# A fused attention and MLP kernel: four slots for the copies of q sums in two batches, and the loads of weights issued from ACT's queue

## The chip, the cores and the metric

The kernel runs on one core of one Trainium2 chip, as one launch. A core has five engines that each work through instructions of their own in program order and meet at semaphores: TensorE (PE in the profile, with its loads of stationary operands as PEld), VectorE (DVE), ScalarE (ACT), GpSimd (POOL) and SyncE (SP), and 16 DMA engines that the queues of the issuing engines feed. The metric is the device time of the launch in microseconds; less is better.

## The reference

Linear attention with exponential features, and then an MLP of two matmuls with a GELU between, in fp32:

```python
def phi(x):                      # q, k: 8 batches, 8 heads, 576 positions, 64 wide
    proj = einsum('bhsd,df->bhsf', x, w_phi)                 # 128 features
    proj = proj - max(abs(proj), axis=-1, keepdims=True)
    return concatenate([exp(proj), exp(-proj)], axis=-1)

kv  = einsum('bhsf,bhsd->bhfd', phi(k), v)
z   = sum(phi(k), axis=2)
num = einsum('bhsf,bhfd->bhsd', phi(q), kv)
den = einsum('bhsf,bhf->bhs', phi(q), z)[..., None] + 1e-06
x   = (num / den), heads side by side                        # 4608 tokens x 512
out = gelu(x @ w_in) @ w_out                                 # 512 -> 2048 -> 512
```

`w_in` and `w_out` are float64, so they reach the chip as 8-byte words and are made into fp32 there.

## The kernel before, in words

**Attention.** A batch is worked in two quads of four heads (`k_quad`, L379) and four pairs of heads (`q_pair`, L459). A quad loads `kt` and `vt`, and for each of five units PE projects k into `pk`, DVE takes the largest absolute value (`mx`, L417) and subtracts it, ACT makes the two exponentials `ek` (L433), and PE adds their products with v up in `kv`, which ACT copies to `kvn`. A pair, for each half of the positions, loads `qt`, projects it to `pq`, ACT copies it to `pc`, GpSimd finds the largest absolute value over the features (`mb`, L499), DVE subtracts it, and ACT makes `ef` (L505). In the first two batches (`b < ND`) PE then computes, for each of the two heads, 65 rows `pn` out of `ef` and `kvn` (64 of the numerator, one of the denominator). ACT copies them to `xo` (L515), and two DMAs write them from there to DRAM, `x_d` (L517) and `d_d` (L519). In later batches the denominator goes through `un` and `db` (L529 to L535) and one copy takes both heads. `quotients` reads the denominators of a half back, inverts them and writes `r_d`.

**MLP.** `block` (L578) takes 256 tokens: it loads `xr` from `x_d` and `rb` from `r_d`, multiplies, splits the product into `xh` and `xl`, and then alternates three matmuls per piece of `w_in` into `ph`, two GELUs on ACT, a difference on DVE (`gl`) and three matmuls per piece of `w_out` into `po`. There are 18 blocks.

**Weights.** 32 tiles of 128 x 512 eight-byte words, 512 KB each, go through `split_weight` (L330). One DMA brings `raw` (L336). ACT takes the absolute value of the upper words (`wt`, L339), DVE clamps, shifts and joins in four steps (L340 to L346), ACT casts the result to `w`, and DVE subtracts for the remainder. `raw` and `w` have a tag of their own each time, so no load waits for a slot; `weights` (L355) lets load number n be issued from n x 3.996 us on in the plan.

**Order.** Each operation is handed to a planner with `op(engine, cost, function, reads, writes, rank)`. `order` (L105) plays a list schedule in which an engine takes, of the operations that could start now, the one of the least rank; the slots of SBUF and PSUM are part of it (a tag has n buffers, taken in turn). `emit` (L240) writes the instructions out in the order of their planned starts. On the chip each engine then keeps that order, and waits where something is late. The first two batches have ranks from -200, the weights from 43.9 on, the blocks from 57.4 on.

Slots of the tags that matter here: `xo` 2, `un` 1, `db` 1 in SBUF (L288), `pn` 1 in PSUM (L290).

Of the kernel before, what the change touches and what calls it, by code (L numbers as in the profile page):

```python
# [10 lines left out]
F32 = mybir.dt.float32  # L11
F32R = mybir.dt.float32r
U32 = mybir.dt.uint32
I64 = mybir.dt.int64
# [13 lines left out]
P = 128  # L28
HS = S // 2
# [29 lines left out]
class Plan:  # L59
# [19 lines left out]
    def op(self, eng, cost, fn, r=(), w=(), also=(), rank=0.0, table=None, late=0.0, kb=0, duty=1.0, kind="f", psum=False):  # L79
        o = Op()  # L80
        o.eng, o.cost, o.fn, o.rank, o.table, o.late, o.n = eng, cost, fn, rank, table, late, len(self.ops)
        o.users, o.ready, o.nbytes, o.duty, o.kind, o.psum = [], self.since, kb, duty, kind, psum
        deps = set()
        for b in r:
            deps.update(b.writers)
        for b in w:
            deps.update(b.writers)
            deps.update(b.readers)
        for b in r:
            b.readers.append(o)  # L90
        for b in w:
            b.writers.append(o)
        o.bufs = list(dict.fromkeys([*r, *w, *also]))
        for b in o.bufs:
            b.left += 1
        o.deps = deps
        o.wait = len(deps)
        for d in deps:
            d.users.append(o)
        if eng == "pe" and self.stream in ("k", "q"):  # L100
            o.rank += PULL
        self.ops.append(o)
        return o

    def order(self, bias):  # L105
# [54 lines left out]
        while len(done) < n:  # L160
# [33 lines left out]
            _, t, o = best  # L194
# [14 lines left out]
            if o.eng == "pool":  # L209
                taken.append([t, t + cost, False])  # L210
            o.start, o.end = t, run(t, cost, o.duty) if o.eng == "pe" else t + cost
            if o.nbytes:
                dge[0] = max(dge[0], t) + 0.55
                dma[0] = max(dma[0], dge[0] + 0.75) + o.nbytes / 350.0
                o.late = dma[0] + 0.15 - o.end
# [60 lines left out]
def fused_kernel(ctx: ExitStack, tc: tile.TileContext, qT, kT, va, w_st, w_in, w_out, out):  # L276
# [53 lines left out]
    def split_weight(src, nm, rank):  # L330
        tag = f"w_{nm}"
        raw = plan.pool(spool, tag, 1)([P, 512, 2], U32, f"raw_{nm}")
        w = plan.pool(spool, tag, 1)([P, 2, 512], F32R, f"w_{nm}")
        t = sb["ob"]([P, 512], U32, f"wt_{nm}")
        k = dict(rank=rank)
        op("sp", 0.06, lambda: nc.sync.dma_start(out=raw().bitcast(I64), in_=src), w=[raw], kb=524, **k)  # L336
        low, high = (lambda: raw()[:, :, 0]), (lambda: raw()[:, :, 1])
        v = nc.vector
        op("act", act(512) + 0.04, lambda: nc.scalar.activation(t().bitcast(F32), high().bitcast(F32), AF.Abs), r=[raw], w=[t], **k)  # L339
        op("dve", dve(512, fast=True), lambda: v.tensor_scalar(  # L340
            out=t().bitcast(F32), in0=t().bitcast(F32), scalar1=F64_MIN, scalar2=F64_MAX, op0=ALU.max, op1=ALU.min), r=[t], w=[t], **k)
        op("dve", dve(512, fast=True), lambda: v.tensor_scalar(
            out=t(), in0=t(), scalar1=3, scalar2=0x3FFFFFF8, op0=ALU.logical_shift_left, op1=ALU.bitwise_and), r=[t], w=[t], **k)
        op("dve", dve(512), lambda: v.scalar_tensor_tensor(  # L344
            out=t(), in0=low(), scalar=29, in1=t(), op0=ALU.logical_shift_right, op1=ALU.bitwise_or), r=[raw, t], w=[t], **k)
        op("dve", dve(512), lambda: v.scalar_tensor_tensor(  # L346
            out=t(), in0=high(), scalar=0xC0000000, in1=t(), op0=ALU.bitwise_and, op1=ALU.bitwise_or), r=[raw, t], w=[t], **k)
        hi = lambda: w()[:, 0, :]
        copy("act", act(512), hi, lambda: t().bitcast(F32), [t], [w], **k)
        tt("dve", dve(512), lambda: w()[:, 1, :], lambda: t().bitcast(F32), lambda: hi().bitcast(F32), ALU.subtract, [t, w], [w], **k)  # L350
        return w
# [107 lines left out]
    def q_pair(b, p, kvs, rank, halves=(0, 1)):  # L459
# [4 lines left out]
        for half in halves:  # L464
# [43 lines left out]
            if b < ND:  # L508

                for j in range(2):  # L510
                    pn = ps["pn"]([P, HS], F32, f"pn_{nm}_{j}")
                    op("pe", 2 * mm4_cost(D + 1, HS), lambda pn=pn, kvn=kvn, ef=ef, j=j: [
                        mm(pn()[: D + 1], lhsT=kvn()[:, 2 * s + j, :], rhs=ef()[:, s, j], start=s == 0, stop=s == 1) for s in range(2)
                    ], r=[kvn, ef], w=[pn], kind="d", **k())
                    xo = sb["xo"]([P, HS], F32, f"xo_{nm}_{j}")  # L515
                    copy("act", act(HS, True), lambda xo=xo: xo()[: D + 1], lambda pn=pn: pn()[: D + 1], [pn], [xo], **k())
                    op("sp", 0.06, lambda xo=xo, x_to=x_to, j=j: nc.sync.dma_start(out=x_to()[64 * j : 64 * j + 64], in_=xo()[:D]),  # L517
                       r=[xo], w=[x_to], kb=74, **k())
                    op("sp", 0.06, lambda xo=xo, d_to=d_to, j=j: nc.sync.dma_start(out=d_to()[2 * p + j : 2 * p + j + 1], in_=xo()[D : D + 1]),  # L519
                       r=[xo], w=[d_to], kb=1, **k())  # L520
                continue
# [167 lines left out]
EPACE = 20.0  # L689
TF = 90.0  # L690
ND = 2
LUMP = 2.5
LINGER = 3.0
PAIR_K = 0.43
# [48 lines left out]
```

## Time and profile before

| | us |
|---|---|
| median of 3 runs | 1156.19 |
| the three runs | 1152.53, 1156.19, 1345.22 |
| the profiled execution | 1154.29 |
| its span, first to last instruction | 1152.5 |
| PE busy in the span | 1114.6 |
| ACT busy | 570.2 |
| DVE busy | 547.5 |
| POOL busy | 317.8 |

Busy times are of the whole span; the opening, in which the weights come in and the first two batches are worked, differs from the rest, so a table by stretches is read beside the page. An instruction that issues a DMA is not counted as busy. Every DMA of this kernel is issued by SP, and the profile tells the length of the issue, not the time until the data has landed. The granted clock is the share of TensorE's full clock that it had in a stretch.

### The profile page before, as it was taken

What the parts mean: (1) busy time and instruction counts of PE and PEld (TensorE: products, weight loads), DVE (VectorE), ACT (ScalarE), POOL (GpSimd) and SP (SyncE); (2) the same over time, 40 slices, a digit from 0 to 9 for tenths busy, and PEclk for the clock granted to TensorE, in tenths of its full rate; (3) what the DMA queues carried; (4) which work ended last, traced back from release to release, by engine and by line L of the source; (5) the groups of instructions that cost most, each with busy time, mean ns of one, the idle gap of its engine ahead of it and who ended that gap; (6) DMA issues with size and microseconds to landing.
All of it is one profiled execution on the core that took longest, in us unless ns stands there. A gap on an engine that the chain in (4) does not pass through costs nothing.

```text
span 1152.5 us, 21902 instructions
## 1 busy us (share of the span) xinstructions
PE 1114.6 (97%) x9096; PEld 930.4 (81%) x9096; DVE 547.5 (48%) x905; ACT 570.2 (49%) x965; POOL 317.8 (28%) x116
## 2 busy tenths in 40 slices
PE   7887999999999999999999999999999999999998
PEld 4554777887887888878888878888899998989997
DVE  5987898454556464444465455545211212122010
ACT  4877667555555565657556555555322222222121
POOL 3323023263435243333453543343300000000000
PEclk8999999999999999999999999999999999999999
DMA  7778623223141413222231321212012011010000
GB/s 264 218 218 240 196 67 84 83 74 101 34 123 50 117 33 108 72 73 73 79 106 56 111 65 32 76 35 76 22 47 55 8 48 48 8 38 19 1 19 19
DMA packets 80852, 92.00 MB, mean 80 GB/s; under 512 B 24736, under 2 KB 67904, under 8 KB 80752
## 3 DMA queue, kind: packets, MB, share of 16 engines
q1 hardware_dynamic: 80752, 90.60, 26.9%
q8 instruction: 71, 1.16, 0.4%
q14 instruction: 29, 0.24, 0.1%
HBM read 71.40 MB, written 19.17 MB: 79 GB/s over the span
## 4 chain that ended last, share of the span: by engine, by line
PE 75%; DVE 4%; POOL 2%; issue 1%; ACT 1%; DMA 0%; SPq 0%; ACTq 0%; POOLq 0%; DVEq 0%
PE po L295 32%; PE ph L295 30%; PE kv L295 4%; PE pn L295 4%; PE pq L295 2%; PE pk L295 2%; POOL mb L499 1%; DVE pc L321 1%; POOL db L534 1%; DVE gl L321 1%; DMA rb<-r_d 0%; DVE mx L417 0%; DVE wt_o L344 0%; ACT pc L315 0%; DVE wt_o L346 0%
## 5 line engine op out<-in xcount | busy, mean ns | idle before, releaser
L295 PE MATMUL ph<-xh,w_i 128*128 128x256 f32 x2304 | 433.8, 283 | 0.5 <-DVE gl L321 0.5
L295 PEld LDWEIGHTS ph<-xh,w_i 128*128 128x128 f32 x2304 | 362.4, 189 | 11.2 <-issue 3.5
L295 PE MATMUL po<-w_o,gh 128*128 128x512 f32 x1152 | 364.8, 398 | 0.0
L295 PE MATMUL ph<-xl,w_i 128*128 128x256 f32 x1152 | 323.7, 281 | 0.0
L321 DVE TENSOR_TENSOR gl<-ph,gh 128x512 fp32r<-128x512 f32 x144 | 98.9, 688 | 326.3 <-ACT ph L622 325.6
L295 PEld LDWEIGHTS po<-w_o,gh 128*128 128x128 f32 x1152 | 209.5, 188 | 48.8 <-ACT gh L621 2.4
L534 POOL PARTITION_ALL_REDUCE db<-un x48 | 175.2, 3649 | 224.7 <-DVE un L531 137.1
L295 PE MATMUL po<-w_o,gl 128*128 128x512 f32 x576 | 229.3, 398 | 6.8 <-DVE gl L321 6.5
L499 POOL PARTITION_ALL_REDUCE mb<-pc x64 | 144.1, 2252 | 281.2 <-ACT pc L315 215.2
L295 PEld LDWEIGHTS ph<-xl,w_i 128*128 128x128 f32 x1152 | 217.6, 189 | 2.8
L621 ACT ACTIVATE gh<-ph 128x512 fp32r<-128x512 f32 x144 | 86.1, 598 | 267.7 <-PE ph L295 267.2
L295 PEld LDWEIGHTS po<-w_o,gl 128*128 128x128 f32 x576 | 108.0, 188 | 37.9 <-DVE gl L321 13.7
L433 ACT ACTIVATE ek<-pk 128x512 f32<-128x512 f32 (+1 forms) x160 | 81.0, 553 | 72.4 <-DVE pk L321 70.9
L295 PEld LDWEIGHTS kv<-vt,ek 128*64 128x64 f32 (+1 forms) x2560 | 85.3, 139 | 35.4 <-ACT ek L433 15.0
L295 PE MATMUL kv<-vt,ek 128*64 128x65 f32 (+1 forms) x2560 | 97.7, 227 | 12.3 <-ACT ek L433 11.1
L295 PE MATMUL pn<-ef,kvn 128*64 128x288 f32 (+1 forms) x512 | 98.0, 425 | 9.9 <-ACT xo L315 7.1
L417 DVE TENSOR_REDUCE mx<-pk 128x4 f32<-128x512 f32 (+1 forms) x80 | 50.5, 632 | 112.8 <-PE pk L295 112.8
L505 ACT ACTIVATE ef<-pc 128x576 f32<-128x576 f32 x128 | 82.2, 681 | 29.6 <-DVE pc L321 29.0
L622 ACT ACTIVATE ph<-ph 128x512 f32<-128x512 f32 x144 | 85.4, 593 | 0.0
L321 DVE TENSOR_TENSOR pc<-pc,mb 128x576 f32<-128x576 f32 x64 | 57.6, 900 | 52.9 <-POOL mb L499 52.6
L295 PEld LDWEIGHTS pn<-ef,kvn 128*64 128x64 f32 (+1 forms) x512 | 38.9, 138 | 45.5 <-ACT xo L315 11.8
L621 ACT ACT_TABLE_LOAD x48 | 61.6, 1283 | 27.0 <-PE ph L295 26.4
(47 smaller groups left out, 768.5 us busy)
## 6 DMA issues: line engine op xcount, KB each, us to landing
qt<-in_qT_dram SPq DMA_DIRECT2D x112, 144.0 KB
vt<-in_va_dram SPq DMA_DIRECT2D x16, 585.0 KB
kt<-in_kT_dram SPq DMA_DIRECT2D x16, 576.0 KB
out_dram<-ob SPq DMA_DIRECT2D x36, 256.0 KB
raw_i<-in_w_in_dram SPq DMA_DIRECT2D x16, 512.0 KB
raw_o<-in_w_out_dram SPq DMA_DIRECT2D x16, 512.0 KB
x_d<-xo SPq DMA_DIRECT2D x48, 144.0 KB
x_d<-xo SPq DMA_DIRECT2D x32, 72.0 KB
```

What stands on the lines that cost most here:

```text
L295: return tc.keep_in_program_order(nc.tensor.matmul(*a, **kw))
L321: op(eng, cost, lambda: e.tensor_tensor(out=dst(), in0=a(), in1=b(), op=o), r=r, w=w, **kw)
L417: op("dve", dve(256 * n, True), lambda xs=xs, mx=mx: nc.vector.tensor_reduce(out=mx()[:, 0].rearrange("p (j i) -> p j i", j=2), in_=xs(), ...
L433: op("act", act(256 * n, True), lambda xs=xs, es=es, s=s: nc.scalar.activation(es[s](), xs(), AF.Exp, scale=1.0 - 2.0 * s), r=[x], w=[e[s] ...
L499: op("pool", 2.2, lambda mb=mb, pc=pc: nc.gpsimd.partition_all_reduce(mb(), pc(), P, bass_isa.ReduceOp.absmax), r=[pc], w=[mb], **k(1))
L505: op("act", act(2 * HS), lambda ef=ef, pc=pc, s=s: nc.scalar.activation(ef()[:, s], pc(), AF.Exp, scale=1.0 - 2.0 * s), r=[pc], w=[ef], ta ...
L534: op("pool", 3.7, lambda db=db, un=un: nc.gpsimd.partition_all_reduce(db(), un(), P, bass_isa.ReduceOp.add), r=[un], w=[db], **k())
L621: op("act", act(2 * TB, True) + 0.016, lambda gh=gh, ph=ph: nc.scalar.activation(gh(), ph(), AF.Gelu), r=[ph], w=[gh], table="gelu", rank= ...
L622: op("act", act(2 * TB, True) + 0.037, lambda ph=ph: nc.scalar.activation(ph(), ph(), AF.Gelu), r=[ph], w=[ph], table="gelu", rank=URGE + rk)
```

## The change

The copies `xo` of the first two batches take their slot in turn from the tags `xo`, `un`, `xo`, `db`, four buffers instead of two, with no new memory. The 32 loads of weights are issued by ACT (`nc.scalar.dma_start`) instead of SP, with a planned cost of 0.1 and a rank that is lower by 300. The planner takes such a load to land a fixed time after its issue, and it takes no share of the planned DMA queue any more.

```diff
--- before.py
+++ after.py
@@ -209,7 +209,9 @@
             if o.eng == "pool":
                 taken.append([t, t + cost, False])
             o.start, o.end = t, run(t, cost, o.duty) if o.eng == "pe" else t + cost
-            if o.nbytes:
+            if o.nbytes and o.eng == "act":
+                o.late = 2.0 + o.nbytes / 150.0
+            elif o.nbytes:
                 dge[0] = max(dge[0], t) + 0.55
                 dma[0] = max(dma[0], dge[0] + 0.75) + o.nbytes / 350.0
                 o.late = dma[0] + 0.15 - o.end
@@ -333,7 +335,7 @@
         w = plan.pool(spool, tag, 1)([P, 2, 512], F32R, f"w_{nm}")
         t = sb["ob"]([P, 512], U32, f"wt_{nm}")
         k = dict(rank=rank)
-        op("sp", 0.06, lambda: nc.sync.dma_start(out=raw().bitcast(I64), in_=src), w=[raw], kb=524, **k)
+        op("act", ISSUE, lambda: nc.scalar.dma_start(out=raw().bitcast(I64), in_=src), w=[raw], kb=524, rank=rank - 300.0)
         low, high = (lambda: raw()[:, :, 0]), (lambda: raw()[:, :, 1])
         v = nc.vector
         op("act", act(512) + 0.04, lambda: nc.scalar.activation(t().bitcast(F32), high().bitcast(F32), AF.Abs), r=[raw], w=[t], **k)
@@ -512,7 +514,7 @@
                     op("pe", 2 * mm4_cost(D + 1, HS), lambda pn=pn, kvn=kvn, ef=ef, j=j: [
                         mm(pn()[: D + 1], lhsT=kvn()[:, 2 * s + j, :], rhs=ef()[:, s, j], start=s == 0, stop=s == 1) for s in range(2)
                     ], r=[kvn, ef], w=[pn], kind="d", **k())
-                    xo = sb["xo"]([P, HS], F32, f"xo_{nm}_{j}")
+                    xo = sb[("xo", "un", "xo", "db")[(2 * half + j) % 4]]([P, HS], F32, f"xo_{nm}_{j}")
                     copy("act", act(HS, True), lambda xo=xo: xo()[: D + 1], lambda pn=pn: pn()[: D + 1], [pn], [xo], **k())
                     op("sp", 0.06, lambda xo=xo, x_to=x_to, j=j: nc.sync.dma_start(out=x_to()[64 * j : 64 * j + 64], in_=xo()[:D]),
                        r=[xo], w=[x_to], kb=74, **k())
@@ -689,6 +691,7 @@
 EPACE = 20.0
 TF = 90.0
 ND = 2
+ISSUE = 0.1
 LUMP = 2.5
 LINGER = 3.0
 PAIR_K = 0.43
```

The planner makes a new order from that, on every engine. Three places of it follow. Names end in a running number that has no meaning; `pc_0_0_1` is batch 0, pair 0, half 1, `ek_0_0_0_1` is batch 0, quad 0, unit 0, sign 1, `raw_i0_0` is a tile of `w_in`, and the lines of the change stand two higher than before.

ACT at the start of the program, before:

```order
L300 ACTIVATE idle_66<-idle_66 128x1
L315 COPY pc_0_0_0_106<-pq_0_0_0_0_95 128x288
L315 COPY pc_0_0_0_106<-pq_0_0_0_1_97 128x288
L433 ACTIVATE ek_0_0_0_1_127<-pk_0_0_0_101 128x512
L315 COPY pc_0_0_1_131<-pq_0_0_1_0_120 128x288
L315 COPY pc_0_0_1_131<-pq_0_0_1_1_122 128x288
L433 ACTIVATE ek_0_0_0_0_137<-pk_0_0_0_101 128x512
L433 ACTIVATE ek_0_0_1_140<-pk_0_0_1_111 128x512 x2
L505 ACTIVATE ef_0_0_0_162<-pc_0_0_0_106 128x576 x2
L339 ACTIVATE wt_i0_0_173<-raw_i0_0_82 128x512
L339 ACTIVATE wt_i1_0_183<-raw_i1_0_91 128x512
```

and now:

```order
L338 DMA raw_i0_0_70<-in_w_in_dram 128x512
L302 ACT_TABLE_LOAD
L302 ACTIVATE idle_66<-idle_66 128x1
L338 DMA raw_i1_0_91<-in_w_in_dram 128x512
L341 ACTIVATE wt_i0_0_94<-raw_i0_0_70 128x512
L338 DMA raw_i2_0_105<-in_w_in_dram 128x512
L317 CAST w_i0_0_112<-wt_i0_0_94 128x512
L317 COPY pc_0_0_0_116<-pq_0_0_0_0_100 128x288
L317 COPY pc_0_0_0_116<-pq_0_0_0_1_102 128x288
L341 ACTIVATE wt_i1_0_125<-raw_i1_0_91 128x512
L317 COPY pc_0_0_1_138<-pq_0_0_1_0_131 128x288
L317 COPY pc_0_0_1_138<-pq_0_0_1_1_133 128x288
```

The first load and the whole conversion of its tile now stand ahead of the first copy `pc`, two more loads are issued before it, and the second conversion begins between the copies of the two halves.

SP where the copies of batch 1 are written out and the first block's `xr` is read (`vt_2_1` is an input of batch 2), before:

```order
L517 DMA x_d1_1_1_1171<-xo_1_1_1_1_1201 64x288
L519 DMA d_d1_1_1038<-xo_1_1_1_1_1201 1x288
L336 DMA raw_o11_1231<-in_w_out_dram 128x512
L469 DMA qt_1_3_1_1240<-in_qT_dram 128x288
L591 DMA xr_0_1188<-x_d0_1_0_445 128x256
L595 DMA rb_0_1190<-r_d0_0_861 64x4x256
L517 DMA x_d1_2_0_1283<-xo_1_2_0_0_1270 64x288
L519 DMA d_d1_0_986<-xo_1_2_0_0_1270 1x288
L336 DMA raw_i0_3_1290<-in_w_in_dram 128x512
L388 DMA vt_2_1_1294<-in_va_dram 128x1170
L591 DMA xr_0_1188<-x_d0_2_0_614 128x256
```

and now:

```order
L519 DMA x_d1_1_1_1206<-xo_1_1_1_0_1201 64x288
L521 DMA d_d1_1_1076<-xo_1_1_1_0_1201 1x288
L471 DMA qt_1_3_0_1215<-in_qT_dram 128x288
L597 DMA rb_0_1174<-r_d0_0_889 64x4x256
L593 DMA xr_0_1172<-x_d0_2_0_664 128x256
L519 DMA x_d1_1_1_1206<-xo_1_1_1_1_1231 64x288
L521 DMA d_d1_1_1076<-xo_1_1_1_1_1231 1x288
L390 DMA vt_2_1_1278<-in_va_dram 128x1170
L593 DMA xr_0_1172<-x_d0_3_0_797 128x256
L471 DMA qt_1_3_1_1290<-in_qT_dram 128x288
L519 DMA x_d1_2_0_1325<-xo_1_2_0_0_1320 64x288
```

The loads of weights between the writes and reads are gone, and the fourth read of `xr_0` now comes ahead of the writes of `xo_1_2`, behind three of which it stood before.

PE where the first matmuls of block 0 stand (`ph_0_0`, `pn_1_3` is the last pair of batch 1), before:

```order
L295 MATMUL kv_2_0_0_1313<-vt_2_0_956,ek_2_0_1_1_1391 64x65 x2
L295 MATMUL pn_1_3_0_1_1426<-ef_1_3_0_1379,kvn_1_1_1_1296 65x288 x2
L295 MATMUL pk_2_0_2_1438<-wst_68,kt_2_0_868 128x128 x2
L295 MATMUL pn_1_3_1_0_1446<-ef_1_3_1_1431,kvn_1_1_1_1296 65x288 x2
L295 MATMUL ph_0_0_1456<-xh_0_1429,w_i0_0_260 128x256
```

and now:

```order
L297 MATMUL kv_2_0_0_1380<-vt_2_0_957,ek_2_0_0_1_1318 64x65 x2
L297 MATMUL kv_2_0_0_1380<-vt_2_0_957,ek_2_0_0_0_1351 64x65 x2
L297 MATMUL kv_2_0_0_1380<-vt_2_0_957,ek_2_0_0_1_1318 64x65 x2
L297 MATMUL pk_2_0_1_1410<-wst_68,kt_2_0_867 128x128 x4
L297 MATMUL ph_0_0_1419<-xh_0_1339,w_i0_0_112 128x256
```

`ph_0_0` stood behind three of the four groups `pn_1_3`; now it and `ph_0_1` stand ahead of all four.

## Rows read from the trace of the kernel before

**Rows 1.** The page, busy time of each engine (us, share of the span, instructions).

```profile
PE 1114.6 (97%) x9096; PEld 930.4 (81%) x9096; DVE 547.5 (48%) x905; ACT 570.2 (49%) x965; POOL 317.8 (28%) x116
```

**Rows 2.** Table by stretches: length, busy PE, PEld, DVE, ACT, POOL, clock, DMA share, GB/s.

```profile
0.00:130.00 130.00, 106.18 (x1158) 67.43 (x1158) 105.34 (x179) 91.11 (x198) 37.62 (x20) 0.95 0.75 231
10.00:130.00 120.00, 98.45 (x1138) 63.78 (x1134) 104.33 (x176) 89.16 (x195) 37.43 (x16) 0.94 0.75 227
30.00:70.00 40.00, 35.22 (x429) 21.83 (x428) 38.65 (x69) 32.63 (x73) 9.86 (x4) 1.00 0.69 209
100.00:110.00 10.00, 7.07 (x72) 3.65 (x68) 8.29 (x13) 7.22 (x17) 5.67 (x3) 1.00 0.91 273
130.00:200.00 70.00, 65.58 (x542) 54.91 (x544) 64.87 (x108) 49.92 (x79) 17.84 (x6) 1.00 0.34 92
200.00:1000.00 800.00, 794.69 (x6460) 674.53 (x6457) 354.43 (x589) 396.55 (x630) 262.37 (x91) 1.00 0.23 66
```

**Rows 3.** Waits from 0 to 130 us (total us, times, longest us).

```profile
PE kv L295 <- ACT ek L433: 8.9, 8, 2.2
...
PE pn L295 <- ACT xo L315: 7.1, 7, 3.2
...
ACT xo L315 <- DMA x_d<-xo: 5.2, 5, 1.9
...
DVE xr L321 <- DMA qt<-in_qT_dram: 3.5, 1, 3.5
...
PE pn L295 <- ACT ef L505: 2.3, 3, 1.2
...
PE kv L295 <- ACT kvn L315: 1.1, 2, 0.7
PE pq L295 <- ACT pc L315: 0.9, 1, 0.9
...
PE pq L295 <- DMA qt<-in_qT_dram: 0.4, 1, 0.4
```

**Rows 4.** Instructions in time order, 87 to 112 us (start, length, [idle before]).

```profile
87.47 0.70 PE L295 MATMUL pn<-ef,kvn 128*65 128x288 f32 x2 [0.72 <-ACT ef L505]
...
104.61 1.27 PE L295 MATMUL pn<-ef,kvn 128*65 128x288 f32 x4 [0.38 <-ACT ef L505]
...
106.28 0.44 SPq L519 DMA_DIRECT2D d_d<-xo  x1
...
107.67 1.19 PE L295 MATMUL pn<-ef,kvn 128*65 128x288 f32 x4 [1.10 <-ACT xo L315]
...
111.62 0.40 ACT L315 COPY xo<-pn 65x288 f32<-65x288 f32 x1 [1.93 <-DMA x_d<-xo]
...
112.07 2.18 PE L295 MATMUL pn<-ef,kvn 128*65 128x288 f32 x4 [3.22 <-ACT xo L315]
```

**Rows 5.** Table by stretches, two of low clock.

```profile
111.00:117.00 6.00, 4.93 (x38) 3.05 (x39) 2.60 (x4) 3.56 (x8) 0.22 (x1) 0.50 0.81 243
22.00:28.00 6.00, 6.00 (x62) 4.19 (x60) 4.88 (x7) 2.11 (x5) 2.43 (x1) 0.50 0.61 227
```

**Rows 6.** One tile's instructions: issues on SP, duration in ns, shortest/median/longest.

```profile
L336 SPq DMA_DIRECT2D raw_i<-in_w_in_dram x16: 328/425/1686, 4.5 to 117.4; - x16
...
L336 SPq DMA_DIRECT2D raw_o<-in_w_out_dram x16: 328/389/434, 11.9 to 134.3; - x16
...
L517 SPq DMA_DIRECT2D x_d<-xo x32: 451/452/1005, 28.5 to 125.1; - x32
```

**Rows 7.** Table by stretches, the instructions on `wt_i` alone: 16 weight conversions.

```profile
0.00:200.00 200.00, 50.77 (x80) 20.40 (x32) 0.97 0.61 182
```

**Rows 8.** Instructions in time order, the first 10 us.

```profile
0.72 0.39 SPq L308 DMA_DIRECT2D wst<-in_w_st_dram  x1
...
2.65 0.23 DVE L317 CAST wd<-wst 128x128 fp32r<-128x128 f32 x1 [1.26 <-DMA wst<-in_w_st_dram]
...
9.54 0.70 ACT L315 COPY pc<-pq 128x288 f32<-128x288 f32 x2 [7.33 <-PE pq L295]
```

## The prediction

> **What bounds the kernel now.** I read the busy line of the page first. PE is busy for 1114.6 of the span's 1152.5 us [rows 1], so there are 38 us in which it does nothing, and a change that leaves the matmuls alone can move only those, and the stretches in which PE runs at a lower clock. The table by stretches says where they lie. From 200 to 1000 us PE is busy for 794.69 of 800 us, from 130 to 200 us for 65.58 of 70, but in the first 130 us for 106.18 of 130: 23.8 us idle [rows 2]. The change touches the first two batches and the loads of weights, which all lie in those 130 us (the last load is issued soon after), so the opening is the stage that decides.
>
> Who ends PE's waits there is in the waits of that window: `ek` 8.9, `xo` 7.1, `ef` 2.3, `kvn` 1.1 and `pc` 0.9 us, all of them written by ACT, 20.3 us together [rows 3]. A DMA ends 0.4 us. Yet ACT is no full engine: from 10 to 130 us it is busy for 89.16 of 120 us, 74%, DVE for 104.33, and from 30 to 70 us DVE for 38.65 of 40 [rows 2]. So work goes DVE, ACT, PE, and ACT is the last link wherever PE stands.
>
> **1. The four slots.** Before, a copy `xo` uses the slot of the copy two before it, and must wait until that one's DMA to DRAM has landed. ACT waits for that 5 times, 5.2 us, at most 1.9 [rows 3]. The worst place is told in time order [rows 4]: the second DMA of a copy is issued at 106.28, the copy that needs its slot starts at 111.62 after 1.93 us of idle, and PE's next `pn` starts at 112.07 after 3.22 us of idle. With four slots the wait is for the copy four before, so it goes. PE's gaps right behind those held copies are 0.72, 0.38, 1.10 and 3.22 us [rows 4]: **−5.4 us**. The low end adds the clock: from 111 to 117 us the granted clock is 0.50, the 1.2 GHz level, with PE busy 4.93 us [rows 5], after the idle of [rows 4]; at the 2.4 GHz level that work takes half, 2.5 us less. I don't take it, because the same fall, at 22 to 28 us [rows 5], stands behind idle that this change leaves. The high end is 0: `pn` has one buffer in PSUM, so the next `pn` waits for the copy in any case, and something else may come last. The borrowed tags `un` and `db` are used by batch 2 on, and the last copy of batch 1 is before those; nothing waits there.
>
> **2. The queue of SP without the weights.** Loads of q and the reads of `x_d` stood behind 512 KB transfers on one queue, while the DMA engines were busy 0.91 of the time at 100 to 110 us [rows 2]. What this cost is 0.4 us of PE [rows 3], and 3.5 us in which DVE waits for the first block's `xr` [rows 3], beside PE that was then working. I take **−0.4 us**, ends −3.9 and 0. The Trainium skill (DMA: Bandwidth & Descriptors, Issuing engines are not separate DMA queues) says that DMAs of all issuing engines run on the same 16 DMA engines, and that a second issuer saves sequencer time alone; by that rule alone this term is 0. No run here has a second queue, so the trace doesn't decide it.
>
> **3. 32 issues in ACT's own order.** On SP an issue of a weight load takes 0.425 us in the median for `raw_i` and 0.389 for `raw_o`, from 0.328 to 1.686 [rows 6]. ACT executes in order, so the next activation stands behind each. If it takes as long there, that is 16 x 0.425 + 16 x 0.389 = 13.0 us of ACT in a stage in which it has 30.8 us idle. Lower bound of what reaches PE: the share of the time in which PE already waits for ACT, 20.3 of 130, 16%, so 2.0 us. Upper bound: the share in which ACT is busy, 74%, so that a delay is passed on: 9.7 us. No row is nearer to either, and I take the middle: **+5.9 us**. SP loses the same issues, which is worth nothing: no wait of PE names SP.
>
> **4. Conversions ahead of attention.** Loads rank 300 higher and arrive earlier, and so the order puts conversions earlier. A conversion takes 20.40 / 16 = 1.28 us of ACT and 50.77 / 16 = 3.17 of DVE [rows 7]. At the start a whole one now stands ahead of the first copy `pc`, which ran at 9.54 [rows 8]. The 64 KB of `wst` were issued at 0.72 and used at 2.65, 1.93 us [rows 8]; 524 KB at the 273 GB/s of 100 to 110 us [rows 2] take 1.9 us more, 3.8 at half of it beside the loads of k and v. So the weights are there at about 4.6 to 6.5, the conversion ends by 9.1 to 11.0, and `pc` moves by 0 to 1.5: **+0.7 us**. Counted in the two orders, ACT at `kvn_0_1_0` has one more first step and two more casts behind it than before; one or two conversions of 3.17 us on a DVE that is 97% busy at 30 to 70 us [rows 2] delay attention by up to 6.3 us. They are missing later, where PE has 4.4 us idle at 130 to 200 us [rows 2]. Ends −4.4 and +6.3, and the middle: **+1.0 us**.
>
> The sum is 1154.3 − 5.4 − 0.4 + 5.9 + 0.7 + 1.0 = **1156 us**, against the profiled execution's 1154.29 (span 1152.5). The median of the three runs is 1.9 us above that execution, and one run of the three is far off, so I leave the number there. All low ends together give 1140, all high ends 1172.
>
> **Rivals.**
>
> Faster: ACT hides the issues in its idle (2.0), the fall of the clock at 111 us goes with its idle (−7.9 in all), and the first block starts earlier (−3.9): 1154.3 − 7.9 − 3.9 + 2.0 + 0.7 = 1145 us. For it: the order puts `ph_0_0` ahead of the last four `pn` groups of batch 1, so PE has block work where it stood still. Against it: that very place makes those `pn` wait in PE's order for `xl_0`.
>
> The slots bring nothing, because the next `pn` waits for something else as long: 1156 + 5.4 = 1161.5 us. For it: only 5.2 of the waits of `xo` are for a DMA. Against it: at 111.62 the DMA is plainly last [rows 4].
>
> The issues are longer on ACT because two issuers meet. Half of an SP issue of 0.452 us [rows 6] each time is 32 x 0.226 = 7.2 us of ACT, 45% of it (the middle of 16 and 74) 3.2 us: 1159 us. For it: SP issues its small writes between the same activations. Against it: nothing, since no row has two issuers. The Trainium skill (Perfetto Trace Analysis, DMA Instruction — HWDGE) describes it: the block that generates descriptors is shared by the issuing sequencers and locked while one uses it.
>
> Slower: a full DMA queue holds ACT. An issue on SP took up to 1.686 us and an `x_d` issue up to 1.005 [rows 6], with the DMA engines 0.75 busy over the stage [rows 2]; SP could afford it. At a mean of 1.005 us ACT loses 32.2 us, more than the 30.8 it has idle, and at 74% that is 23.9 in place of 5.9: 1174 us. Every 0.1 us of the mean above 0.41 costs 2.4; above 1.14 us the kernel is slower by over 2%; at 1.686 each it would be 1190. Against it: the medians stand near the shortest.
>
> **How the numbers follow.** My forecast has 0.40, the faster rival 0.22, the idle slots 0.16, the meeting of issuers 0.12, the held ACT 0.10. The range 1145 to 1168 leaves out the held ACT and the far half of the faster rival. 2% is 23 us, about what a measurement can tell here: less than all idle of PE in the opening. Faster by that needs all of it (0.02); slower needs issues of over 1.14 us (0.04); the rest is 0.94.
>
> **What would show it.** Right: no `xo` ended by `x_d`; ACT busy about as before, but with raw issues between its activations, 0.33 to 0.45 us each; PE idle in the first 130 us still 20 to 27 us, more of it ended by `ek` and `ef`; the first `ph` before 119 us; the same times per block after 200 us, shifted. Wrong: issues above 0.6 us on ACT; `wt_i` or `pc` waiting for a load; low clock in other stretches than the two; PE idle at 200 to 1000 us other than about 5 us, which no term here has.

## The result: 1% slower, and the profile after

The changed kernel takes 1166.21 us in the median of 6 runs (1161.41 to 1168.08), beside 1155.19 us for the kernel before in the same comparison: a ratio of 1.0098, 95% interval [1.0073, 1.0123]. One run of the kernel before, 1345.22 us, is far off the others (1151.42 to 1157.90) and is in no ratio. No change was forecast, at 1156; the time lies inside the range, near its upper end. The profiled execution took 1165.13 us, its span is 1163.3, against 1154.29 and 1152.5.

The page of the changed kernel, busy times and the DMA queues (packets, MB, share of 16 engines), answers to [rows 1]:

```profile
PE 1120.8 (96%) x9096; PEld 935.3 (80%) x9096; DVE 541.7 (47%) x905; ACT 565.7 (49%) x961; POOL 317.6 (27%) x116
...
q10 hardware_dynamic: 4608, 16.78, 4.5%
```

PE's idle time is 1163.3 - 1120.8 = 42.5 us, 4.6 more than before; its busy time is 6.2 us longer with as many instructions. `q10` is new: the loads on their own queue. The table by stretches of the changed kernel (columns as in [rows 2]):

```profile
0.00:130.00 130.00, 105.69 (x1073) 67.47 (x1074) 104.62 (x176) 89.83 (x190) 36.94 (x20) 0.88 0.70 223
130.00:200.00 70.00, 68.03 (x549) 57.04 (x549) 58.15 (x102) 48.02 (x76) 10.79 (x4) 0.98 0.42 110
...
300.00:600.00 300.00, 292.91 (x2626) 243.38 (x2625) 160.21 (x275) 169.60 (x274) 131.79 (x46) 0.99 0.28 80
600.00:1000.00 400.00, 397.33 (x2989) 343.44 (x2989) 150.65 (x244) 166.44 (x270) 100.02 (x35) 1.00 0.19 53
```

and the two late stretches of the kernel before, which [rows 2] hold only together:

```profile
300.00:600.00 300.00, 297.91 (x2589) 246.83 (x2587) 158.77 (x270) 176.58 (x276) 126.07 (x43) 1.00 0.28 80
600.00:1000.00 400.00, 399.06 (x3013) 345.84 (x3013) 146.76 (x236) 164.05 (x267) 96.17 (x33) 1.00 0.18 51
```

Two things are new. First the clock of the opening: a mean of 0.88, where [rows 2] have 0.95. With the two levels 1.2 and 2.4 GHz that is 2 x 0.12 x 130 = 31 us at the lower one, against 13. Second the middle: from 300 to 1000 us PE is idle for 7.09 + 2.67 = 9.8 us, against 2.09 + 0.94 = 3.0. The opening's idle time is 24.3 us, 23.8 before: no change there. Three of the stretches at the lower clock, from the same view:

```profile
51.70:55.10 3.40, 3.40 (x51) 3.00 (x50) 3.40 (x7) 2.20 (x4) 0.00 (x0) 0.51 0.75 282
82.50:92.70 10.20, 7.72 (x49) 4.44 (x50) 9.99 (x17) 7.12 (x16) 4.46 (x2) 0.50 0.60 179
533.00:536.40 3.40, 3.40 (x9) 2.62 (x8) 2.00 (x5) 0.59 (x2) 1.25 (x1) 0.50 0.58 173
```

In the first two PE is busy for 11.1 of 13.6 us, 82%, so the 18 us more at half speed are worth about 18 x 0.82 / 2 = 7.4 us (an estimate); the one at 533 adds 1.7, the middle's idle 6.7, the opening's idle 0.5, and from 130 to 200 us PE is idle 2.4 us less. That makes 13.9 us for a span that is 10.8 longer; the 3 us between stay open. PE's own work, estimated as its busy time less half of what it is busy at the lower clock, comes to 1103.9 us against 1106.9 before, but the run `e1_slots_only`, with the order of before, has 1105.6: part of it is what two traces of one order differ by.

Who ends the waits, 0 to 130 us, beside [rows 3]:

```profile
PE kv L297 <- ACT ek L435: 11.6, 7, 3.1
PE pq L297 <- ACT pc L317: 3.4, 2, 3.0
PE pn L297 <- ACT ef L507: 2.7, 1, 2.7
...
PE pn L297 <- ACT xo L317: 1.0, 3, 0.5
```

The wait for `xo` went from 7.1 to 1.0 us, and `ek` and `pc` took its place: 8.9 to 11.6 and 0.9 to 3.4. Term 1 forecast the first, but most of it is not the slots' doing: the run `e2_act_only` below, with this order and two slots, has

```profile
PE pn L297 <- ACT xo L317: 2.5, 7, 0.5
```

**The issues on ACT.** One tile's instructions (duration in ns, shortest/median/longest), and 11.8 to 13.3 us in time order:

```profile
L338 ACTq DMA_DIRECT2D raw_i<-in_w_in_dram x16: 334/335/404, 0.7 to 120.2; - x16
L338 ACTq DMA_DIRECT2D raw_o<-in_w_out_dram x16: 334/334/347, 13.2 to 137.4; - x16
```

```profile
11.81 0.60 ACT L435 ACTIVATE ek<-pk 128x512 f32<-128x512 f32 x1 [0.31 <-DVE pk L323]
11.82 0.33 ACTq L338 DMA_DIRECT2D raw_i<-in_w_in_dram  x1
12.31 1.08 ACT L435 ACTIVATE ek<-pk 128x512 f32<-128x512 f32 x2
13.19 0.33 ACTq L338 DMA_DIRECT2D raw_o<-in_w_out_dram  x1
13.26 0.62 ACT L435 ACTIVATE ek<-pk 128x512 f32<-128x512 f32 x1
```

An issue runs beside an activation: the pair of `ek` behind the first issue starts 0.50 us after the `ek` ahead of it, and the `ek` behind that pair 0.95 us later, 0.48 for each. Behind 29 of the 32 issues the next activation follows without idle time. So the 0.33 us of an issue are not added to ACT's time, as term 3 has it. One issue did hold ACT, by a wait ahead of it that its length doesn't show:

```profile
131.59 0.33 ACTq L338 DMA_DIRECT2D raw_o<-in_w_out_dram  x1
132.05 0.39 ACT L317 COPY xo<-pn 65x288 f32<-65x288 f32 x1 [2.11 <-DMA xr<-x_d]
```

The load starts as soon as the read of `xr` has landed, by the profile's semaphore events, and `xo` stands behind it. Why it waits for that read the trace doesn't tell.

**Two places where PE waits long.** In the opening, the instructions of DVE, ACT and PE about 82 us:

```profile
80.65 0.18 DVE L556 TENSOR_SCALAR dc<-dc 128x18 f32<-128x18 f32 x1 [1.91 <-DMA dc<-d_d]
...
81.25 0.63 DVE L323 TENSOR_TENSOR w_o<-wt_o,w_o 128x512 fp32r<-128x512 f32 x1
...
81.91 0.67 ACT L341 ACTIVATE wt_o<-raw_o 128x512 f32<-128x512 f32 x1 [2.55 <-DVE w_o L323]
...
82.48 0.68 ACT L317 COPY pc<-pq 128x288 f32<-128x288 f32 x2
...
82.92 1.63 PE L297 MATMUL pq<-qt,wst 64*128 64x288 f32 x4 [3.04 <-ACT pc L317]
```

Read from the top: DVE stands still until a denominator has come back from DRAM, with the end of a conversion behind it in its order; ACT stands at the next conversion, which needs that slot, with `pc` behind it; PE stands at `pq`, which needs the place that `pc` empties. Then the clock falls for 10.2 us. In the middle, about 531 us:

```profile
526.96 2.22 POOL L501 PARTITION_ALL_REDUCE mb<-pc  x1
...
527.90 0.59 ACT L624 ACTIVATE ph<-ph 128x512 f32<-128x512 f32 x1
...
529.21 0.76 DVE L323 TENSOR_TENSOR pc<-pc,mb 128x576 f32<-128x576 f32 x1 [3.25 <-POOL mb L501]
529.89 1.22 DVE L323 TENSOR_TENSOR xr<-xr,rb 128x1024 f32<-128x1024 f32 x1
...
531.02 0.68 DVE L323 TENSOR_TENSOR gl<-ph,gh 128x512 fp32r<-128x512 f32 x1
...
531.76 0.19 PEld L297 LDWEIGHTS po<-w_o,gl 128*128 128x128 f32 x1 [2.87 <-DVE gl L323]
531.76 0.50 PE L297 MATMUL po<-w_o,gl 128*128 128x512 f32 x1 [2.42 <-DVE gl L323]
```

`gl` had its inputs from 528.5 on, but in DVE's order it stands behind `pc`, which waits 3.25 us for GpSimd, and behind `xr`. PE waits 2.42 us. The same shape, an instruction that PE needs behind one that waits for GpSimd or a DMA, stands at 425, 465, 478 and 608 us.

### The profile page after: what moved, and what is told of

It reads as the page before. It is cut to its first block, busy times and chain, and to the rows that moved or that the text cites. A ratio compares the mean times of both kernels' runs of the same rounds, so it can differ in the third digit from the quotient of the medians.

```text
span 1163.3 us, 21920 instructions
## 1 busy us (share of the span) xinstructions
PE 1120.8 (96%) x9096; PEld 935.3 (80%) x9096; DVE 541.7 (47%) x905; ACT 565.7 (49%) x961; POOL 317.6 (27%) x116
## 5 line engine op out<-in xcount | busy, mean ns | idle before, releaser
L297 PE MATMUL kv<-vt,ek 128*64 128x65 f32 (+1 forms) x2560 | 100.4, 231 | 12.4 <-ACT ek L435 12.3
L323 DVE TENSOR_TENSOR pc<-pc,mb 128x576 f32<-128x576 f32 x64 | 55.2, 863 | 58.0 <-POOL mb L501 57.7
```

What stands on the lines that cost most here:

```text
L297: return tc.keep_in_program_order(nc.tensor.matmul(*a, **kw))
L323: op(eng, cost, lambda: e.tensor_tensor(out=dst(), in0=a(), in1=b(), op=o), r=r, w=w, **kw)
```

## Experiments

All ratios are to the kernel before in the same comparison, five rounds where nothing else is said. "New order" is the changed kernel's order of instructions, "old order" that of before.

| run | order | loads on | ratio | 95% interval | median us |
|---|---|---|---|---|---|
| the change | new | ACT | 1.0098 | 1.0073 to 1.0123 | 1166.21 |
| `e1_slots_only` | old | SP | 0.9997 | 0.9981 to 1.0012 | 1151.42 |
| `e2_act_only` | new | ACT | 1.0119 | 1.0095 to 1.0143 | 1166.31 |
| `e3_old_order_act_queue` | old | ACT | 1.0052 | 1.0026 to 1.0077 | 1158.38 |
| `e4_new_order_sp_queue` | new | SP | 1.0119 | 1.0098 to 1.0141 | 1165.64 |
| `e5_later` (3 rounds) | another | ACT | 1.0160 | 1.0132 to 1.0187 | 1170.65 |
| `e6_new_dummies` (3) | new | ACT | 1.0178 | 1.0145 to 1.0212 | 1172.60 |
| `e7_old_dummies` (3) | old | SP | 1.0055 | 1.0036 to 1.0074 | 1158.41 |
| `e8_no_rank` (3) | another | ACT | 1.0180 | 1.0156 to 1.0203 | 1171.55 |
| `e9_new_then_old` | new to 250 us, then old | SP | 1.0155 | 1.0132 to 1.0177 | 1169.26 |
| `e10_old_then_new` | old to 250 us, then new | SP | 1.0030 | 1.0016 to 1.0045 | 1154.14 |
| `e11_gl_ahead` | new, 5 moves | ACT | 1.0063 | 1.0037 to 1.0088 | 1158.88 |
| `e12_old_then_new_gl_ahead` | as `e10`, 5 moves | SP | 0.9962 | 0.9945 to 0.9979 | 1147.37 |
| `e13_dc_later` | as `e11`, `dc` later | ACT | 1.0023 | 1.0008 to 1.0038 | 1154.80 |
| `e14_dc_later_mx_ahead` | as `e13`, one more | ACT | 1.0024 | 1.0008 to 1.0039 | 1154.36 |
| `e15_old_then_new_dc_later` | as `e12`, `dc` later | SP | 0.9936 | 0.9911 to 0.9960 | 1144.52 |

### The change taken apart: slots, queue, order

**The slots alone.**

```diff
-                    xo = sb["xo"]([P, HS], F32, f"xo_{nm}_{j}")
+                    xo = sb[("xo", "un", "xo", "db")[(2 * half + j) % 4]]([P, HS], F32, f"xo_{nm}_{j}")
```

> Half the change: four slots for the copies, loads still on SP. The instruction order of every engine is that of the kernel before, row for row, so only the waits for the DMA of the copy two before can go. Theory O (the new order makes the kernel slower, by stretches at the 1.2 GHz level): 1147 to 1153 us, since the 5.2 us of those waits and part of the low clock from 110 to 117 us go. Theory Q (the second queue makes it slower): the same. Theory S (the slots are of no use, another wait follows): 1153 to 1157 us.

They are worth nothing that can be measured: 0.9997. The 1151.42 us lie in the range of Theory O and Q, but the kernel before took 1152.40 in that comparison, so Theory S is the one borne out. ACT no longer waits for `x_d`, but PE is still idle for 22.3 of the first 130 us, where it was 23.8. It waits for `xo` all the same, and the wait for the first `gl` is longer (1.8 us at 131 us before):

```profile
PE pn L295 <- ACT xo L315: 6.0, 8, 1.9
PE po L295 <- DVE gl L321: 3.4, 1, 3.4
```

**The loads alone**, the change with the slots of before.

```diff
-                    xo = sb[("xo", "un", "xo", "db")[(2 * half + j) % 4]]([P, HS], F32, f"xo_{nm}_{j}")
+                    xo = sb["xo"]([P, HS], F32, f"xo_{nm}_{j}")
```

> The other half: loads on ACT with the new rank and price, two slots. Its instruction order is that of the changed kernel, row for row. Theory O: 1163 to 1172 us, with 30 us or more at the granted clock of 0.5. Theory Q: 1163 to 1172 us as well. If the slots were what makes it slower: 1150 to 1157 us.

All of the loss is here: 1166.31 us, as both theories said. The next two separate what this part does: the queue that issues, and the order that the planner makes of it.

**Old order, ACT's queue**: the kernel before, with one word changed.

```diff
-        op("sp", 0.06, lambda: nc.sync.dma_start(out=raw().bitcast(I64), in_=src), w=[raw], kb=524, **k)
+        op("sp", 0.06, lambda: nc.scalar.dma_start(out=raw().bitcast(I64), in_=src), w=[raw], kb=524, **k)
```

> The loads are issued from ACT, but planned as before, so every other instruction stands in the order of the kernel before; two slots. Theory O: 1150 to 1157 us, about 17 us at a clock of 0.5 as before, since an issue on ACT costs nothing there. Theory Q (issues in ACT's order and loads that share the DMA engines with the rest cost time): 1160 to 1166 us. My recorded sum, 5.9 us for the issues: 1160 us.

**New order, SP's queue**: the change, with one word changed back.

```diff
-        op("act", ISSUE, lambda: nc.scalar.dma_start(out=raw().bitcast(I64), in_=src), w=[raw], kb=524, rank=rank - 300.0)
+        op("act", ISSUE, lambda: nc.sync.dma_start(out=raw().bitcast(I64), in_=src), w=[raw], kb=524, rank=rank - 300.0)
```

> Planned as in the changed kernel, with its four slots, but the loads are issued from SP: the order of all other instructions is that of the changed kernel. Theory O: 1161 to 1170 us, with 30 us or more at a clock of 0.5. Theory Q: 1150 to 1157 us.

The new order without any issue on ACT is 1.2% slower; with the issues it is 1.0% slower, and the intervals overlap. So in the change the queue costs nothing on balance, and the order is enough for all of the loss. On balance, since SP's queue has a price of its own here: ACT waits 7.7 us for loads in the first 130 us of `e4`, 2.3 in the change.

In the old order ACT's queue costs 0.5%, some 6 us, with runs from 1153.65 to 1167.57. That lies between the ranges of the two theories, and near the 1160 us of my recorded sum. Part of it is seen in the profiled execution of `e3`, on ACT and then on PE:

```profile
105.39 0.65 ACT L315 CAST w_o<-wt_o 128x512 fp32r<-128x512 f32 x1
108.36 0.33 ACTq L336 DMA_DIRECT2D raw_i<-in_w_in_dram  x1
108.75 0.60 ACT L433 ACTIVATE ek<-pk 128x512 f32<-128x512 f32 x1 [2.70 <-DMA rb<-r_d]
110.16 0.51 PE L295 MATMUL kv<-vt,ek 128*64 128x65 f32 x10 [2.71 <-ACT ek L433]
```

The issue itself waits until another DMA, the read of `rb`, has landed, `ek` stands behind it in ACT's order, and PE waits 2.71 us for `ek`. A second issue holds ACT for 1.65 us at 136 us. What makes up the rest of the 6 us stays open. For the queue I had the Trainium skill (DMA: Bandwidth & Descriptors, Issuing engines are not separate DMA queues), by which a second issuer brings no bandwidth; these runs agree in that neither order gained from it beyond its interval.

### What of the order? Three theories tried

**Conversions ahead of attention.** If they are the harm, later loads help.

```diff
-                plan.since = WPACE * n
+                plan.since = WPACE * n + 9.0
```

> The changed kernel, but each load may be issued only 9 us later in the plan, so that conversions fall back to about where they stood before the change; queue, slots, price and rank as in the change. If conversions ahead of attention are what costs: 1151 to 1158 us, and a low clock of 10 to 20 us in the first 135 us instead of 34. If it is ACT's queue, or any order other than the tuned one: 1160 to 1168 us.

It is slower than the change, although the first conversion starts at 14.9 us, as before (15.2; 5.0 in the change). But this is a new order of its own, so it speaks against the theory without ruling it out. From 130 to 200 us PE is busy for 60.04 of 70 us, and the waits of 0 to 200 us show one cause: an `xo` that PE waits 7.1 us for.

```profile
PE kv L297 <- ACT ek L435: 11.6, 10, 2.1
PE pn L297 <- ACT xo L317: 10.7, 7, 7.1
```

**The rank alone.**

```diff
-        op("act", ISSUE, lambda: nc.scalar.dma_start(out=raw().bitcast(I64), in_=src), w=[raw], kb=524, rank=rank - 300.0)
+        op("act", ISSUE, lambda: nc.scalar.dma_start(out=raw().bitcast(I64), in_=src), w=[raw], kb=524, rank=rank)
```

> The changed kernel without the rank lowered by 300: loads of ACT have the rank of their conversions, and only the planner's new price (a fixed time to land, no share of the DMA queue) is left. Its order is near that of the change. If the price makes the bad order: 1160 to 1168 us. If the rank does: 1151 to 1157 us.

It is slower still than was expected of either. The planner's new price of a load is enough to make a slower order; the 300 lower rank is not needed.

**The clock.** Both kernels with 96 matmuls more in the first two batches, which compute nothing that is used and keep PE busy where it waits for `ek`:

```diff
+                        if b < EB and new:
+                            ins += [mm(acc()[:, 384:512], lhsT=wst(), rhs=wst(), start=first, stop=True, skip_group_check=True) for _ in range(4)]
```

> The changed kernel with 96 idle matmuls (128 x 128, into columns of the bank of kv that nobody reads) ahead of the 24 groups of kv that wait for ek; the order of all else is unchanged. They wait for nothing, so PE works in the gaps. Theory C (the low clock that follows the gaps is a cost of its own): low clock in the first 135 us falls from 34 us to under 20, and the time to 1156 to 1163 us, though there is more work. Rival D (the clock only follows, DVE and ACT set the end of the opening): 1165 to 1172 us even where the clock stays high.

> The kernel before with the same 96 idle matmuls. Theory C: its two low stretches of 6.8 us in the first 120 us shrink, 1146 to 1152 us. Rival D: 1153 to 1160 us, by the work added.

The clock of 0 to 130 us (the third number from the end) was held in both, first the new order and then the old:

```profile
0.00:130.00 130.00, 117.22 (x1262) 83.83 (x1262) 107.20 (x175) 89.35 (x189) 37.41 (x20) 0.99 0.71 222
```

```profile
0.00:130.00 130.00, 119.88 (x1320) 85.31 (x1321) 104.01 (x171) 88.01 (x193) 36.05 (x20) 0.99 0.73 223
```

Neither became faster, which is nearer to Rival D than to Theory C. That alone doesn't show that the lower clock costs nothing, because the added matmuls are work themselves: PE's own work, estimated as above, is 1128.2 us instead of 1103.9 in the new order and 1129.5 instead of 1106.9 in the old. Its idle time and what the lower clock took of it fall by nearly as much, together by 22.6 and 20.4 us.

What speaks against the clock is the distance of the two orders: 1.0178 to 1.0055, 1.2%, where it is 1.0 to 1.2% without. The two traces speak the other way: idle and lost time in the first 300 us are 1.8 us apart in them, against 5.3 in the change and the kernel before, and the rest lies between 300 and 1000 us (12.7 against 3.0). But the profiled execution of `e6`, 1166.88 us, is the fastest of its four (up to 1174.82). So whether the 7.4 us are a cost of their own, or lie where PE would wait anyway, stays open.

### Where in the program

The two plans joined at 250 us: the instructions that one plan starts before that time in its order, all the others in the order of the other (four slots, loads on SP).

```diff
+        head = [o for t, n, o in plans[first] if t < until]
+        have = {o.n for o in head}
+        other = "new" if first == "old" else "old"
+        self.done = head + [o for t, n, o in plans[other] if n not in have]
```

> Loads on SyncE's queue and the four slots, as in the run with the new order on SP's queue (1.012 times the kernel before). The instructions that the change's plan starts before 250 us stand in its order; all the others follow in the order of the plan of before. Theory M (the middle decides: in the trace of the change PE is idle for 9.8 us between 300 and 1000 us where it was 3.0, nearly all behind gl of DVE, and the clock falls once there, 3.4 us at half speed): the middle's 8 us go, 1153 to 1158 us, ratio 1.002 to 1.005, PE idle at 300 to 1000 us about 3. Theory P (the opening decides: more PE gaps and twice the low clock before 140 us): 1162 to 1167 us, ratio 1.009 to 1.013. Rival X (an order is only good as a whole, the seam costs as much as either): 1165 us or more.

> The other half: the instructions that the plan of before starts before 250 us stand in that order, all the others follow in the order of the change's plan. Loads on SyncE's queue, four slots. Theory M (the middle decides): the waits for gl between 300 and 700 us are all there, 1158 to 1162 us, ratio 1.006 to 1.009, PE idle at 300 to 1000 us 8 to 10 us, the opening's low clock as before (17 us). Theory P (the opening decides): 1150 to 1154 us, ratio 0.998 to 1.003. Rival X: 1165 us or more.

The first came out as Rival X and tells little: at the seam PE waits 6.1 us for one `ef`, and from 200 to 300 us it is busy for 89.98 us where the change has 97.95. The second is cleaner. Its 1.0030 is the upper end of Theory P and outside of Theory M: the opening decides. The new middle costs 1.0030 against 0.9997 with the old one (`e1_slots_only`, of another comparison), some 4 us, and the waits for `gl` are back. That leaves some two thirds of the loss to the opening. Waits of PE from 300 to 700 us, before, the change, and this run:

```profile
PE po L295 <- DVE gl L321: 2.0, 4, 0.7
```

```profile
PE po L297 <- DVE gl L323: 7.7, 6, 2.4
```

```profile
PE po L321 <- DVE gl L347: 7.1, 6, 2.4
```

### The wait itself: five instructions moved

These two runs take those waits away and leave all else. Each pair is an instruction of DVE that waits and the `gl` behind it; all of DVE from the one to the other goes behind the `gl`.

```diff
+        for late, first in AHEAD:
+            i, j = seq.index(at[late]), seq.index(at[first])
+            held = [o for o in seq[i:j] if o.eng == "dve"]
+            seq[i : j + 1] = [o for o in seq[i : j + 1] if o not in held] + held
```

> The change as it is, except that at five places between 420 and 610 us a gl of DVE, which po of PE waits for, is moved ahead of the DVE instructions in front of it that wait for something else (the subtraction pc that waits for GpSimd's mb, the multiplication xr that waits for its read from DRAM, dc that waits for d_d). In the trace of the change these five waits cost PE 1.16, 1.20, 0.72, 2.42 and 1.75 us, 7.25 together, and the clock falls once behind them (3.4 us at half speed, 1.7 us). Theory M (a third or more of the loss is this middle): 1157 to 1161 us, ratio 1.003 to 1.006, PE idle at 300 to 1000 us 2 to 4 us instead of 9.8. Rival W (the wait only moves: what was moved back is then late for PE): 1164 to 1168 us, ratio 1.009 to 1.013.

> The same five moves in the run whose opening, to 250 us, has the order of before, and whose middle has the order of the change (ratio 1.003; loads on SyncE's queue, four slots). Theory M: the middle's waits for gl go from 11 us to about 4, and this is as fast as the kernel before or faster: 1145 to 1151 us, ratio 0.995 to 1.000. Rival W: 1153 to 1157 us, ratio 1.002 to 1.005.

Both bear it out. The ratio goes from 1.0098 to 1.0063, just above what Theory M expected, and from 1.0030 to 0.9962; the intervals of the first two overlap, those of the second two lie apart. The waits of 300 to 700 us in the two runs:

```profile
PE po L306 <- DVE gl L332: 1.2, 2, 0.7
```

```profile
PE po L330 <- DVE gl L356: 1.2, 2, 0.7
```

In the first PE is idle for 2.12 + 0.95 = 3.1 us from 300 to 1000 us, as before the change. What was moved back made nothing late that PE waited for: Rival W fell.

The two runs also price the opening. They were compared with each other and have the same five moves; they differ in the order of the first 250 us, and in the queue of the loads, which cost nothing in the new order. The new opening takes 1158.88 us and the old one 1147.37: 11.5 us, 1.0%, near all that the change lost. And the new middle with its five moves is faster than the old one (0.9962 against 0.9997), so the moves win more than those waits had cost.

### The same wait in the opening

`dc` of the first two batches, which waits for DRAM, 4 us later in the plan with what depends on it; then also two steps of a conversion behind `mx` and `pk` at 47 us; then the first in the fastest run.

```diff
+        for o in [o for o in seq if o.eng == "dve" and o.start < 250.0 and o.bufs[0].tag == "dc"]:
+            i = seq.index(o)
+            j = next(j for j in range(i, len(seq)) if seq[j].start > o.start + 4.0)
...
+            seq[i:j] = [q for q in seq[i:j] if q not in held] + [q for q in seq[i:j] if q in held]
```

> The run with the five gl moved ahead (ratio 1.006), and in the first two batches the denominators dc, which DVE reads back from DRAM, stand a few instructions later in DVE's order (4 us in the plan), together with the write of r_d. In the traces of the change and of that run, DVE stands still for 1.9 to 2.0 us at dc around 79 us with conversions queued behind it; ACT then waits 2.5 us for a conversion's end ahead of pc, PE waits 3.0 to 3.1 us for that pc, and the clock is at 0.5 for 10.2 us right there. Theory Q (a DMA wait placed ahead of the conversions is what is left in the opening): that gap and most of that low clock go, 3 us and 3 to 5 us, so 1150 to 1154 us, ratio 0.998 to 1.002. Rival R (DVE is full there and only swaps what is late): 1157 to 1161 us, ratio 1.004 to 1.008.

> The same, and besides two steps of one conversion (wt_o3) stand behind mx and pk of batch 0, quad 1, where PE waits 3.1 us for ek at 47 to 50 us. Conversions ahead of attention are priced at their own length: the two steps take 0.65 and 0.43 us on DVE, so that gap shrinks by 1.1 us, and with it the low clock of 3.4 to 6.8 us behind it may go (up to 3 us). Expected against the run without this move: 1 to 4 us faster, ratio to before 0.995 to 1.001; if DVE's order there doesn't matter, the same within 1 us.

> The fastest run so far (opening in the order of before, middle in the order of the change with the gl moved ahead, ratio 0.996), with the four dc of the first two batches a few instructions later. DVE waits 3.8 us for d_d there, once for 2.0 us ahead of a gl that PE waits 2.7 us for. Theory Q: 2 to 4 us faster, 1142 to 1146 us, ratio 0.991 to 0.995. Rival R: the same, 0.995 to 0.998.

`e13` comes to 1.0023, between the two expectations and nearer to Theory Q; `e14` adds nothing, where 1 to 4 us were expected; `e15` goes from 0.9962 to 0.9936 in the order of before, as Theory Q said (the intervals overlap), so the wait for `dc` is no fault of the new order alone. The profiled execution of `e13` shows only part of it: from 0 to 130 us,

```profile
PE kv L314 <- ACT ek L452: 12.4, 7, 3.4
PE pq L314 <- ACT pc L334: 2.7, 2, 1.8
```

the 3.1 us for `pc` went, but an `ek` four us later now waits 3.4 where it was 2.1, and the span is 1153.3 against 1153.5. The gain stands in the medians (1154.80 and 1158.88, of different comparisons), not in the traces; that of `e11` is of one of its fastest executions (1155.26, of 1154.60 to 1162.20). So Q is likely, not shown.

What is left of the opening's loss is not the 0.2% to the kernel before but the distance to `e15`, which has the same moves behind the old opening and was compared with `e13`: 1154.80 against 1144.52 us, 0.9%. From 0 to 130 us, `e13` and then `e15`, and the wait for `ek` in `e15`:

```profile
0.00:130.00 130.00, 105.22 (x1076) 67.83 (x1077) 106.22 (x178) 91.18 (x193) 36.94 (x20) 0.90 0.72 227
0.00:130.00 130.00, 110.54 (x1233) 73.05 (x1234) 113.05 (x195) 96.30 (x207) 37.52 (x20) 0.97 0.79 246
PE kv L340 <- ACT ek L478: 8.1, 8, 2.2
```

In the new opening PE is idle for 24.8 us instead of 19.5, it is at the lower clock for 2 x 0.10 x 130 = 26 us instead of 8, and it waits 12.4 us for `ek` instead of 8.1. What in the order makes `ek` late there, no run shows.

`e15_old_then_new_dc_later` is faster than both kernels: 0.9936 of before. It has the opening of before, the middle of the change with five `gl` moved ahead, `dc` later, and the loads on SP.

## Why the prediction was wrong

**The step that failed is term 4**, with the sentence that came from it, "the same times per block after 200 us, shifted". I priced the new order as conversions ahead of attention in the opening, +0.7 and +1.0 us with +6.3 as the high end. The new order costs 1.19% (`e4`), some 14 us. The first part didn't come: the weights were there at 4.97 us, inside the estimate, and the first `pc` starts at 9.43 us, 9.54 before. The rest is an order that is new on every engine, far beyond the opening, made from a changed price of 32 loads.

What the runs showed in its place has two parts. In the middle, for which no term had a price, `gl` stands behind instructions of DVE that wait for GpSimd or a DMA; that costs a third of a per cent (`e10`), and it is shown, since moving five `gl` ahead takes the waits and the time away. In the opening the new order costs 0.9 to 1.0% (`e11` beside `e12`, `e13` beside `e15`), which is 10.3 to 11.5 us and above the high ends of term 4, 1.5 and 6.3. There PE waits longer for `ek` and is longer at the lower clock, and the cause of that stays open: it may still be conversions ahead of attention, then mis-sized, for `e5` made another order and `e14` moved only two steps.

My list of what would prove me wrong had three of the signs, "low clock in other stretches than the two", "PE idle at 200 to 1000 us" and a `wt_i` that waits for a load (2.3 us), but no term had a price for them. The three places of the order that I compared lie all before 130 us; the middle of DVE's order was never read.

**Term 3** (+5.9 us, bounds 2.0 and 9.7) has the right size in the old order, by luck: some 6 us (`e3`, 3.0 to 8.9). In the change's own order it is about 0 (1.0098 with the issues on ACT, 1.0119 without). The durations were near (0.334 us against 0.389 to 0.425), but an issue on ACT runs beside the activation ahead of it, so the mechanism was wrong; what is seen of the cost is an issue that itself waits for an earlier DMA. The lower bound assumed that an issue stops the engine; no row of before showed an issue on ACT, and the bound should have gone to 0.

**Term 1 was mis-sized**: −5.4 us, measured −0.3 (`e1`, −2.2 to +1.4). ACT's wait for `x_d` went, as described, but PE's wait for `xo` only from 7.1 to 6.0. Two of the four gaps added up, 0.72 and 0.38 us, end with `ef` and not with a copy [rows 4]. The rival that the slots bring nothing had the right mechanism, "something else may come last". In the change's order term 1 and term 3 were wrong by as much in opposite directions, which left the sum looking sound.

**Term 2** (−0.4) can hardly be seen: PE waits 0.3 us for `qt` where it was 0.4, and DVE still waits for the first block's `xr`, 3.9 us where it was 3.5. Of the rivals, the issuers' meeting did not happen: SP's `x_d` issues keep their median of 452 ns, and no issue of a weight on ACT takes over 404. The held ACT happened once, for 2.1 us at 132 us, and not by a long issue; besides, ACT waits for one load, 2.3 us. The rival on the slower side had the sign and not the cause. Last, I took 2% for about what a measurement can tell here; the intervals are within 0.35% to either side, and 1% stands clear of them.

## What to carry to other kernels

Where a planner writes the order, an edit of a price is an edit of every in-order engine: compare the two orders over the whole program, and look on each engine for an instruction that the bounding engine needs and that now stands behind one which waits for a slow engine or a DMA. A new order can be tested apart from what caused it, by keeping the order and undoing the edit, and mended by moving single instructions. Judge a mend beside a run that has the same mend and the other order, not beside the kernel before, which lacks the mend. And a test that adds work, like the added matmuls, has to count that work before its result is read.

## What the runs showed of the hardware

A DMA issue on ACT took 0.334 us in the median and ran beside an activation: behind 29 of 32 issues the next activation followed without idle time. But an issue that waited for an earlier DMA held the activations behind it, for 2.1 us in the change and for 2.7 and 1.65 us in `e3`. Issued from SP, the same loads took 0.389 to 0.425 us in the median. With 96 matmuls more, TensorE's clock stayed at 0.99 of full speed over the opening, and both orders became slower, with some 23 to 24 us of work more (an estimate from busy time and clock).
